# Windowed attention and token/channel mixing on one core: the addition of 1e-9 to the softmax sums moves from VectorE to GpSimd

## The chip, the cores and the metric

The kernel runs on one core of a Trainium2 chip. The metric is the device time of one execution in microseconds (us). A core has five engines that run their own instruction queues in order and wait for one another by semaphores: TensorE (PE in the profile; PEld are its weight loads), VectorE (DVE), ScalarE (ACT), GpSimd (POOL) and SyncE (SP), which here issues most DMAs.

## The reference

Attention with a causal window of 64 over 8 batches, 8 heads, 576 positions and a head size of 64; its output x goes through a token-mixing and a channel-mixing product, each with a residual. All in float32.

```python
scores = scale * np.matmul(q, k.transpose(0, 1, 3, 2))
mask = (rel >= 0) & (rel < window)
scores = np.where(mask, scores, -1000000000.0)
scores = scores - np.max(scores, axis=-1, keepdims=True)
attn = np.exp(scores)
attn = attn / (np.sum(attn, axis=-1, keepdims=True) + 1e-09)
x = np.matmul(attn, v)                     # then heads are joined: batch, position, 512
h = np.maximum(xt @ w_tok1, 0.0) @ w_tok2  # xt: x with positions last
u = x + h.transpose(0, 2, 1)
h2 = np.maximum(u @ w_ch1, 0.0) @ w_ch2
return u + h2
```

## The kernel before

The positions of a batch are cut into nine blocks of 64. A tile is two such blocks, 128 rows for the 128 partitions; there are NT = 36 tiles, nine for each pair of batches, and tile 4 of each nine holds the last block of both batches. The weights arrive as 64-bit floats and are turned into 32-bit ones on the chip, a piece of up to 128x384 at a time (a job). Products that need full precision are done with operands split in two, hi and lo.

The kernel is written in two stages. The first, up to about 290 us, is one loop over i = -1 to 36, in which several tiles are in work at once: scores of tile i+1, softmax of tile i+1, transposition and attention output of tile i, first token product of tile i-1, second token product for earlier tiles, and jobs. The second stage, some 600 us, is the channel product, in which TensorE works almost without a gap. The order on each engine's queue is that of the program text; nothing is reordered.

What an iteration puts on the queues, as far as it bears on the change:

- **VectorE**, in order: softmax(i+1, 0), that is e (L259, scores times scale plus mask) and nm (L262, the negated maximum), or for tiles below 7 only nm (L256) and its scaling (L257); then recip(i) (L297 and L298); the first half of a job's conversion, job_convert_a, L165 to L167 (for i below 4 it stands behind the next softmax half); softmax(i+1, 1); hlo (L345) where a batch's first token product ends; the conversion's second half, L176, L178, L179; and norm(i), x (L303), which multiplies the attention output by the reciprocal ri. For i below 4, norm(i-1) stands ahead of recip(i). In iterations 4 to 6 the weight t2 is split on VectorE too (t2lo, L92), right behind recip(i).
- **GpSimd**, in order: in job_finish the lo part of a weight (t1lo or w1lo, L92), for i below 4 the lo part of an x (split_x, xlo, L92), w (L181, the last addition of a conversion), and from i = 3 on, at the tail of the iteration, split_x of tile i: xlo (L92), or for tile 4 of nine two instructions of L315. split_x waits for ScalarE's hi part, and that for x.
- **ScalarE**: copies of transposed scores (L279), hi parts (L89, L314), the exponentials (L270) with their sums, copies of the token product (L380). softmax_exp(i, 1), which completes the sums of tile i, is issued in iteration i-1, ahead of that iteration's tail.

sm holds the eight sums of each row of a tile (128x8), ri its reciprocals; ri has two buffers. The jobs run in all iterations but those where i mod 9 is 5, and a few listed by hand.

Of the kernel before, what the change touches and what calls it, by code (L numbers as in the profile page):

```python
# [72 lines left out]
def mixer_kernel(ctx: ExitStack, tc: tile.TileContext, qh, kh, vh, wt1, wt2, wc1, wc2, out):  # L73
    nc = tc.nc
# [36 lines left out]
    with ExitStack() as actx:  # L111
# [182 lines left out]
        def recip(i):  # L294
            _, sm = st.pop(i)
            ri = pa.tile([P, H], F32, name=f"ri{i}", tag="ri", bufs=2)
            nc.vector.tensor_scalar_add(ri, sm, 1e-9)  # L297
            nc.vector.reciprocal(ri, ri)  # L298
            return ri

# [135 lines left out]
        for i in range(-1, NT + 1):  # L436
# [24 lines left out]
            if 0 <= i < NT:  # L461
                ri = recip(i)
# [165 lines left out]
```

## Time and profile before

| | |
|---|---|
| time, median of 3 runs | 893.15 us (892.65 to 893.91) |
| the profiled execution, its own time | 894.62 us |
| its span, first to last instruction | 892.5 us |
| mean granted TensorE clock | 0.994 |
| GpSimd busy | 129.3 us (14%) |

The profile is of one execution. Its page gives the busy time of each engine; the span in slices; the chain of work that ended last, followed back from the last instruction; and the costliest groups of instructions by line, with the tile that is written and the one that is read (ri<-sum). A row in order of time starts with the start and the duration in us, then engine, line, operation, tiles and shape; a bracket at its end gives how long the engine had been idle before it and for whom it waited. An instruction can start a few hundredths before the one ahead of it on its engine has ended. A row of the chain gives start, length and what was on the chain then. Busy time of an instruction includes time in which it was started but could not proceed.

### The profile page before, as it was taken

To read this page: it belongs to the slowest core of one execution; us is meant where nothing else is said; L and a number is where in the kernel's file an instruction comes from. 1 tells how busy PE (TensorE), PEld (TensorE's weight loads), DVE (VectorE), ACT (ScalarE), POOL (GpSimd) and SP (SyncE) were. 2 spreads that over 40 slices of the span, in tenths; PEclk is the share of its full clock that TensorE was granted. 3 is DMA by queue.
4 is the path that set the end of the run, shared out by engine and by line. 5 is a ranking of instruction groups with operands and counts; after the bars stand their busy time and mean duration, and the time that the engine had idled before them with its cause. 6 is when DMAs were issued, how large, how long until landed. Compare 5 with 4: busy or idle time off the path is not lost.

```text
span 892.5 us, 14591 instructions
## 1 busy us (share of the span) xinstructions
PE 864.8 (97%) x6002; PEld 706.3 (79%) x6002; DVE 381.5 (43%) x686; ACT 304.9 (34%) x953; POOL 129.3 (14%) x130
## 2 busy tenths in 40 slices
PE   6889999999999979999999999999999999999998
PEld 4667777778778758888888888888888888888887
DVE  4979979988885781130130130220230220220211
ACT  5778778787785240130120120120120120220210
POOL 2434444443332450000000000000000000000000
PEclk9989999999999999999999999999999999999999
DMA  9556667677736330200200200100100100200001
GB/s 324 184 202 242 214 231 241 205 232 261 247 137 196 110 109 24 70 1 24 71 0 32 63 1 35 59 1 36 59 0 36 59 13 24 59 12 35 1 12 36
DMA packets 41490, 87.05 MB, mean 98 GB/s; under 512 B 5456, under 2 KB 19408, under 8 KB 39504
## 3 DMA queue, kind: packets, MB, share of 16 engines
q1 hardware_dynamic: 39312, 84.29, 28.3%
q10 hardware_dynamic: 2112, 1.84, 0.6%
q8 instruction: 47, 0.77, 0.3%
q14 instruction: 19, 0.16, 0.1%
HBM read 65.27 MB, written 20.84 MB: 96 GB/s over the span
## 4 chain that ended last, share of the span: by engine, by line
PE 79%; DVE 14%; ACT 4%; issue 1%; DMA 1%; SPq 0%; POOL 0%; DVEq 0%; ACTq 0%
PE op L586 33%; PE gp L552 30%; PE up L375 4%; PE s L242 3%; PE xp L289 3%; PE h L333 3%; ACT e L270 2%; DVE nm L262 2%; DVE e L259 2%; PE up L368 2%; DVE c L176 2%; PE pp L277 2%; DVE c L165 1%; DVE c L167 1%; ACT pt L279 1%
## 5 line engine op out<-in xcount | busy, mean ns | idle before, releaser
L556 ACT ACTIVATE ghi<-gp 128x512 fp32r<-128x512 f32 x108 | 64.4, 598 | 454.3 <-PE gp L552 453.9
L552 PE MATMUL gp<-uhi,w1hi 128*128 128x512 f32 x432 | 169.1, 392 | 6.4 <-DVE glo L557 6.4
L586 PE MATMUL op<-glo,w2hi 128*128 128x512 f32 (+1 forms) x444 | 170.2, 383 | 0.0
L586 PE MATMUL op<-ghi,w2lo 128*128 128x512 f32 (+1 forms) x444 | 170.2, 383 | 0.0
L586 PE MATMUL op<-ghi,w2hi 128*128 128x512 f32 (+1 forms) x444 | 170.2, 383 | 0.0
L552 PE MATMUL gp<-ulo,w1hi 128*128 128x512 f32 x432 | 168.8, 391 | 0.0
L552 PE MATMUL gp<-uhi,w1lo 128*128 128x512 f32 x432 | 168.7, 390 | 0.0
L557 DVE SCALAR_TENSOR_TENSOR glo<-gp,ghi 128x512 fp32r<-128x512 f32 x108 | 74.4, 690 | 190.4 <-ACT ghi L556 190.3
L588 DVE TENSOR_TENSOR uf<-op,uf 128x512 f32<-128x512 f32 (+1 forms) x37 | 25.1, 677 | 262.2 <-PE op L586 262.2
L552 PEld LDWEIGHTS gp<-uhi,w1hi 128*128 128x128 f32 x432 | 81.5, 189 | 25.2 <-DVE glo L557 8.3
L270 ACT ACTIVATE e<-e,nm 128x128 f32<-128x128 f32 x232 | 90.4, 392 | 25.0 <-DVE nm L262 23.6
L586 PEld LDWEIGHTS op<-glo,w2hi 128*128 128x128 f32 x444 | 83.4, 188 | 16.4
L586 PEld LDWEIGHTS op<-ghi,w2hi 128*128 128x128 f32 x444 | 83.4, 188 | 16.4
L586 PEld LDWEIGHTS op<-ghi,w2lo 128*128 128x128 f32 x444 | 83.4, 188 | 16.4
L552 PEld LDWEIGHTS gp<-uhi,w1lo 128*128 128x128 f32 x432 | 81.5, 189 | 17.0
L552 PEld LDWEIGHTS gp<-ulo,w1hi 128*128 128x128 f32 x432 | 81.4, 188 | 16.8
L181 POOL TENSOR_TENSOR w<-r,c 128x384 f32<-128x384 f32 (+1 forms) x39 | 38.6, 991 | 142.2 <-DVE r L179 116.3
L289 PEld LDWEIGHTS xp<-v,pt 128*64 128x64 f32 x1152 | 39.4, 139 | 21.0 <-ACT pt L279 8.7
L289 PE MATMUL xp<-v,pt 128*64 128x64 f32 x1152 | 47.1, 229 | 5.9 <-ACT pt L279 5.2
L279 ACT COPY pt<-pp 128x512 f32<-128x512 f32 x72 | 41.7, 583 | 14.7 <-PE pp L277 14.5
L242 PE MATMUL s<-k,q 64*64 64x128 f32 x1152 | 44.4, 288 | 1.3 <-DMA k<-kh 0.6
L277 PE MATMUL pp<-ident,e 128*128 128x128 f32 x288 | 45.3, 287 | 0.0
(70 smaller groups left out, 1024.2 us busy)
## 6 DMA issues: line engine op xcount, KB each, us to landing
v<-vh SPq DMA_DIRECT2D x36, 512.0 KB, 3.9
raw<-wc SPq DMA_DIRECT2D x32, 384.0 KB, 4.4
q<-qh SPq DMA_DIRECT2D x36, 256.0 KB, 4.3
k<-kh SPq DMA_DIRECT2D x7, 1280.0 KB, 7.9
out<-uf SPq DMA_DIRECT2D x35, 256.0 KB, 2.3
uf<-u_dram SPq DMA_DIRECT2D x8, 1024.0 KB, 5.8
u_dram<-u SPq DMA_DIRECT2D x7, 512.0 KB, 4.4
w_dram<-w SPq DMA_DIRECT2D x10, 192.0 KB, 3.8
```

The costliest lines, as they stand in the source:

```text
L181: nc.gpsimd.tensor_add(w, rf, cf)
L242: nc.tensor.matmul(s[u][half * BLK:(half + 1) * BLK, j], qt[r, j, half], kbs[b][r, j, n * BLK:n * BLK + P], start=not on_pe, stop=True, sk ...
L270: nc.scalar.activation(e[:, h], src[:, h], AF.Exp, bias=nm[:, g:g + 1], scale=by, accum_out=sm[:, g:g + 1])
L277: nc.tensor.transpose(pp[:, h], e[:, h], ident)
L279: nc.scalar.copy(pt, pp)
L289: nc.tensor.matmul(xp[half * BLK:(half + 1) * BLK, h], pts[h % 2][:, h // 2, half * BLK:(half + 1) * BLK], vt[:, half, h], start=True, sto ...
L333: nc.tensor.matmul(h_ps[b][tt], w[r, slot * DT + tt * P:slot * DT + (tt + 1) * P], x[r], start=first and n == 0, stop=last and n == len(co ...
L375: nc.tensor.matmul(up[:, :n], hx[:, cs], w[:, tt * S + s0:tt * S + s0 + n], start=False, stop=(k == 6), skip_group_check=True)
L552: nc.tensor.matmul(gp, w[:, ct * F + ft * P:ct * F + (ft + 1) * P], x[:, ct], start=(k == 0), stop=(k == 3 * NCT - 1))
L556: nc.scalar.activation(ghi, gp, AF.Relu)
L557: nc.vector.scalar_tensor_tensor(out=glo, in0=gp, scalar=0.0, in1=ghi.bitcast(F32), op0=ALU.max, op1=ALU.subtract)
L586: nc.tensor.matmul(op, w[:, ft, cs], x[:, cols], start=(k == 0), stop=(k == 3 * NFT - 1))
```

## The change

The addition of 1e-9 to the sums is issued on GpSimd; the reciprocal stays on VectorE and now reads what GpSimd wrote. The order in which the program issues the instructions is the same.

```diff
         def recip(i):
             _, sm = st.pop(i)
             ri = pa.tile([P, H], F32, name=f"ri{i}", tag="ri", bufs=2)
-            nc.vector.tensor_scalar_add(ri, sm, 1e-9)
+            nc.gpsimd.tensor_scalar_add(ri, sm, 1e-9)
             nc.vector.reciprocal(ri, ri)
             return ri
```

## The prediction

> **What bounds the kernel now.** I read the page's first parts, then the busy time by stretch, then the line that the change touches, then VectorE (DVE) and GpSimd (POOL) side by side in order of time. From the page: span, PE's busy time, and the chain that ended last by engine.
>
> ```profile
> span 892.5 us, 14591 instructions
> PE 864.8 (97%) x6002; PEld 706.3 (79%) x6002; DVE 381.5 (43%) x686; ACT 304.9 (34%) x953; POOL 129.3 (14%) x130
> PE 79%; DVE 14%; ACT 4%; issue 1%; DMA 1%; SPq 0%; POOL 0%; DVEq 0%; ACTq 0%
> ```
>
> TensorE is the bound on the whole, but 14% of the chain runs over VectorE. The stretches say where (columns: length, then busy time of PE, PEld, DVE, ACT, POOL with their instructions, granted clock, DMA share, GB/s).
>
> ```profile
> 20.00:40.00 20.00, 17.47 (x249) 13.10 (x246) 18.93 (x43) 15.63 (x62) 9.26 (x10) 1.00 0.71 235
> 84.00:114.00 30.00, 29.12 (x365) 23.70 (x368) 28.49 (x54) 22.86 (x88) 13.16 (x13) 1.00 0.63 206
> 146.00:168.00 22.00, 21.26 (x272) 17.23 (x268) 20.86 (x40) 16.94 (x64) 9.00 (x9) 1.00 0.68 238
> 170.00:280.00 110.00, 107.22 (x1338) 86.03 (x1337) 91.29 (x184) 84.39 (x308) 40.09 (x35) 1.00 0.63 207
> ```
>
> From 20 to 40 us VectorE is the fuller engine (95% against 87%): a shorter VectorE helps there. From 84 to 114 and 146 to 168 us both are at about 95% or more: a later VectorE delays TensorE there, an earlier one gains little. From 170 us TensorE (97%) leads and VectorE has 17% of slack. The moved line is in none but these stages. Its own two lines (duration min/median/max in ns):
>
> ```profile
> L297 DVE TENSOR_SCALAR ri<-sum x36: 155/438/922, 14.8 to 271.0; 128x8 f32<-128x8 f32 x36
> L298 DVE RECIPROCAL ri<-ri x36: 202/203/205, 15.0 to 271.6; 128x8 f32<-128x8 f32 x36
> ```
>
> The addition needs 0.155 us and often takes three times that; the reciprocal never takes longer. Iteration i = 12 shows why. In order of time, VectorE, then GpSimd, then the last piece of the sums on ScalarE:
>
> ```profile
> 100.22 0.69 DVE L262 TENSOR_REDUCE nm<-e 128x4 f32<-128x512 f32 x1
> 100.82 0.75 DVE L297 TENSOR_SCALAR ri<-sum 128x8 f32<-128x8 f32 x1
> 101.61 0.20 DVE L298 RECIPROCAL ri<-ri 128x8 f32<-128x8 f32 x1
> 101.73 1.00 DVE L165 TENSOR_SCALAR c<-raw 128x384 int32<-128x384 int32 x1
> 102.76 0.36 DVE L166 TENSOR_SCALAR c<-c 128x384 f32<-128x384 f32 x1
> ...
> 100.25 1.29 POOL L92 TENSOR_TENSOR xlo<-x,xhi 128x512 fp32r<-128x512 f32 x1 [0.25 <-ACT xhi L89]
> 101.50 1.01 POOL L92 TENSOR_TENSOR w1lo<-w,w1hi 128x384 fp32r<-128x384 f32 x1
> ...
> 98.95 0.18 ACT L270 ACTIVATION_READ_ACCUMULATOR e<-e,nm 128x1 f32 x1
> ```
>
> GpSimd's xlo ends at 101.54, and only then does L297 get through (end 101.57). L165 then waits in the same way for w1lo (ends 102.51 and 102.73). The reduction and the reciprocal pass GpSimd unhindered. So most of L297's time is a wait for GpSimd, and that wait doesn't go away by handing the addition to GpSimd: there it stands **behind** the same xlo, because the tail of iteration i-1 issues split_x(i-1) before recip(i) is reached.
>
> **The change part by part.** *The addition on GpSimd.* Its inputs are there: the sums of tile 12 are complete at 99.13, before xlo starts. It can start when the instruction ahead of it ends, even 0.04 us earlier (w1lo starts at 101.50, xlo ends at 101.54). No row shows a 128x8 tensor_scalar on GpSimd, so its cost a is bounded by these (mean ns of one behind the bar):
>
> ```profile
> L92 POOL TENSOR_TENSOR xlo<-x,xhi 128x512 fp32r<-128x512 f32 x32 | 41.3, 1289 | 27.2 <-ACT xhi L89 27.0 <-DVE ri L298 0.3
> L92 POOL TENSOR_TENSOR t1lo<-w,t1hi 128x320 fp32r<-128x320 f32 x4 | 3.5, 869 | 7.2 <-ACT t1hi L89 7.2
> masks.py:199 POOL TENSOR_SCALAR_AFFINE_SELECT ident<-ident 128x128 f32<-128x128 f32 x1 | 0.3, 292 | 0.1
> L615 POOL MEMSET const-float32-0.0<- 128x1 f32 x1 | 0.1, 98 | 0.2 <-issue 0.2
> ```
>
> Below, the memset of one element: 0.10 us. Above, the select over 128 elements: 0.29 us. The two subtractions give (1289-869)/192 = 2.19 ns an element and 169 ns at none, so 186 ns at eight elements. I take a = 0.19, and 0.10 to 0.29 for the range. Less than nothing is out: it is an instruction more on a queue that runs in order.
>
> *The added wait.* The reciprocal now waits for GpSimd. From the end of xlo to the next engine takes 0.05 us (row 41.27 below, after xlo's end at 41.22). With E for the end of xlo, the reciprocal starts at E - 0.04 + a + 0.05 = E + 0.20; it started at E + 0.07. Behind it on VectorE stand the conversion L165 to L167, the second half's softmax, L176 to L179 and x (L303), for which the next xhi, xlo and TensorE wait. Behind the addition on GpSimd stand the split of a weight (w1lo, t1lo) and w (L181); TensorE needs w1lo only in the last stage, so of these only VectorE's own waits for GpSimd count.
>
> *Iterations where w1lo follows at once.* w1lo moves back by a - 0.04 = 0.15 us, and L165, which ends after it, with it: 0.15 later each. Where that lies on the chain of waits, L165 appears in it with its 0.9 us: six times (i = 9, 11, 12, 13, 19, 20), first and last here, and once (i = 18) L166.
>
> ```profile
> 78.26 0.95 DVE c L165
> ...
> 148.19 1.06 DVE c L166
> ...
> 163.99 0.94 DVE c L165
> ```
>
> Six times 0.15 is **+0.90**. At i = 18 the reciprocal comes 0.10 later, and L165 may then lose its place ahead of w1lo, which costs up to a whole L165 (0.3): I take **+0.2**. In the other iterations either nm lasts longer than xlo (0.1 earlier or later, with slack) or TensorE leads: 0.
>
> *Iterations 4 and 5.* Here L297 slips in before xlo has got going, and the addition will have to wait for all of it. VectorE, GpSimd, and the chain's row for TensorE:
>
> ```profile
> 40.12 0.20 DVE L298 RECIPROCAL ri<-ri 128x8 f32<-128x8 f32 x1
> 40.79 0.84 DVE L92 TENSOR_TENSOR t2lo<-w,t2hi 128x384 fp32r<-128x384 f32 x1 [0.47 <-ACT t2hi L89]
> 48.02 1.36 DVE L92 TENSOR_TENSOR t2lo<-w,t2hi 128x384 fp32r<-128x384 f32 x1 [1.31 <-ACT t2hi L89]
> 57.03 0.56 DVE L92 TENSOR_TENSOR t2lo<-w,t2hi 128x384 fp32r<-128x384 f32 x1 [0.28 <-ACT t2hi L89]
> ...
> 39.95 1.27 POOL L92 TENSOR_TENSOR xlo<-x,xhi 128x512 fp32r<-128x512 f32 x1 [0.24 <-ACT xhi L89]
> 47.68 1.28 POOL L315 TENSOR_TENSOR xlo<-x,xlo 64x512 fp32r<-64x512 f32 x1
> ...
> 41.27 1.42 PE h L333 x5
> ```
>
> The reciprocal goes from 40.12 to E + 0.20 = 41.42. t2lo behind it waited for xlo anyway and ended at 41.63, 0.41 after E. Now it starts 0.12 after the reciprocal (as L165 at 101.73 after 101.61) and needs its undisturbed 0.56: E + 0.88. That is 0.47 later, and the same at i = 5 (E = 48.96, end 49.38): **+0.94** together.
>
> *Iterations 0 to 3.* Here recip(i) stands before this iteration's GpSimd work, so the addition is done in time and VectorE is spared 0.19 (27.66 to 27.85). Whether that counts depends on the waits behind it:
>
> ```profile
> 22.19 0.60 DVE L257 TENSOR_SCALAR nm<-nm 128x4 f32<-128x4 f32 x1
> 23.05 1.27 DVE L166 TENSOR_SCALAR c<-c 128x320 f32<-128x320 f32 x1
> 27.66 0.15 DVE L297 TENSOR_SCALAR ri<-sum 128x8 f32<-128x8 f32 x1
> 27.85 0.20 DVE L298 RECIPROCAL ri<-ri 128x8 f32<-128x8 f32 x1
> 28.64 1.17 DVE L257 TENSOR_SCALAR nm<-nm 128x4 f32<-128x4 f32 x1
> 30.08 0.33 DVE L166 TENSOR_SCALAR c<-c 128x320 f32<-128x320 f32 x1
> ...
> 22.71 1.43 POOL L92 TENSOR_TENSOR xlo<-x,xhi 128x512 fp32r<-128x512 f32 x1
> 28.51 1.28 POOL L92 TENSOR_TENSOR xlo<-x,xhi 128x512 fp32r<-128x512 f32 x1
> ```
>
> At i = 2 the scaling L257 comes at 28.64, just after xlo has begun at 28.51, and loses a microsecond. 0.19 earlier it falls before xlo, as at i = 1, where it ended at 22.79 and L166 took the wait instead, ending 0.18 after xlo (24.32 against 24.14). Worked so, xlo ends at about 29.94 and L166 at 30.12 instead of 30.41: 0.29 gained; the same at i = 3. At i = 1 the split ahead of xlo holds L257 either way, at i = 0 VectorE waits for TensorE afterwards: 0. Together **-0.58**.
>
> [...]
>
> *Sum:* 0.90 + 0.20 + 0.94 - 0.58 = **+1.46 us**, on a profiled execution of 894.62 us (span 892.5), which is 0.16% above the median of 893.15. Carried to the median: **894.6**. With a = 0.10: 6 x 0.06 + 2 x 0.38 + 0.1 - 0.58 = +0.6; with 0.29: 6 x 0.25 + 2 x 0.57 + 0.36 - 0.58 = +2.4. So this case's own range is 893.7 to 895.6.
>
> **The rivals.** *The addition is dear.* If one small GpSimd instruction and its signal take about 0.5 us, near the middle between the select's 0.29 and the 0.87 of a 128x320 subtraction, each of the eight places costs 0.31 more and i = 18 its 0.36: +4.1, 897.3. It tips over the 0.2% from a = 0.24 on. For it: no row has this operation. Against: the memset's 98 ns.
>
> *Nothing is gained early.* The wait only moves from L257 to L166 and VectorE's iteration stays as long as it is. For it: at i = 1, where the wait sits on L166 (1.27), VectorE loses as much to GpSimd as at i = 2 on L257 (1.17). Then +2.04: 895.2.
>
> *Iterations 4 and 5 hide it.* If TensorE's h matmuls, which wait for the same xlo (41.27), and not t2lo set the end there, the 0.94 goes: +0.5, 893.7.
>
> *Faster.* If the addition got done before nm ends also in the six iterations, the reciprocal would follow nm at 100.82; L165 would get in at xlo's end as L257 did at 22.79, and L166 would end 0.18 after w1lo, itself pushed from 102.51 by the 0.15 that xlo took longer at 22.71 (1.43, not 1.28), at 102.84 instead of 102.76 + 0.36 = 103.12. Six times 0.28 and the 0.58, without the loss at 4 and 5: -2.2, 891.0. It decides where xlo ends before nm. Against: at i = 12 xlo ends 0.63 after nm, and GpSimd's order is as written.
>
> **How the numbers follow.** 0.2% (1.8 us: below 891.4, above 894.9) is about what this kernel's runs can tell from no change. The forecast case 0.48 (0.28 within the bound, 0.20 above), dear 0.20 (slower), nothing early 0.09 (0.07 slower), hidden 0.11 (within), faster 0.12. Faster 0.12, same 0.41, slower 0.47. The range reaches down to 892.3, between hidden and faster, and up to 897.5, past the dear case.
>
> **What would show it.** On GpSimd 36 instructions of 0.1 to 0.3 us, in iterations 6 to 34 right behind xlo; VectorE's L298 idle before it "<-POOL ri"; at i = 9 to 13 L298 0.1 to 0.2 us after xlo's end and L165 as late; at i = 4 and 5 t2lo at 0.56 us but ending 0.9 after xlo; at i = 2 and 3 L257 at 0.2 to 0.4 us and L166 at over a microsecond. Wrong is the prediction if the additions take 0.4 us or more, if VectorE's iterations from 84 to 114 us get no longer, or if the time moves after 300 us, where nothing was changed.

## The result, and the profile after

The changed kernel takes 902.84 us (median of 4 runs, 901.69 to 903.75), the kernel before 893.53 us beside it (892.65 to 894.79): a ratio of 1.0102 with a 95% interval of 1.0083 to 1.0122. The change costs 9.3 us where 1.5 was forecast, and the time lies above the predicted range. Three single executions among those below (2933.52 us of the kernel before, 1697.85 and 4783.19 us of two kernels with fill, the last of them that kernel's profiled one) ran in a slow state and are left out of the ratios.

From the page of the changed kernel, its span and its engines' busy times:

```profile
span 899.9 us, 14590 instructions
PE 868.0 (96%) x6002; PEld 707.6 (79%) x6002; DVE 367.6 (41%) x650; ACT 304.4 (34%) x953; POOL 138.8 (15%) x166
```

The profiled execution took 901.69 us; against the 894.62 of the profiled execution before it shows 7.07 of the 9.3 us. VectorE has lost 36 instructions and 13.9 us of busy time, and the kernel is longer. Before, the 36 additions were started for 15.6 us in all, where 36 undisturbed ones of 0.155 would take 5.6: most of what VectorE got rid of was time spent started and waiting, and it waits still, now outside an instruction. The two lines of the change, with what VectorE sat idle for ahead of the reciprocal (us, times):

```profile
L297 POOL TENSOR_SCALAR ri<-sum x36: 232/233/237, 13.3 to 280.7; 128x8 f32<-128x8 f32 x36
L298 DVE RECIPROCAL ri<-ri x36: 186/203/204, 14.9 to 281.0; 128x8 f32<-128x8 f32 x36
...
  POOL ri L297: 31.5, 29
```

Those 31.5 us are not the loss: some 10 of them were waited before too, inside L297, and others lie where they cost nothing (2.43 us in iteration 14, whose x is no later than that of 13). The loss is how much later the reciprocal and what follows it come. Iteration 12, VectorE, then GpSimd, in order of time:

```profile
102.34 0.69 DVE L262 TENSOR_REDUCE nm<-e 128x4 f32<-128x512 f32 x1
104.08 0.20 DVE L298 RECIPROCAL ri<-ri 128x8 f32<-128x8 f32 x1 [1.05 <-POOL ri L297]
104.20 1.16 DVE L165 TENSOR_SCALAR c<-raw 128x384 int32<-128x384 int32 x1
...
102.44 1.29 POOL L92 TENSOR_TENSOR xlo<-x,xhi 128x512 fp32r<-128x512 f32 x1 [0.25 <-ACT xhi L89]
103.82 0.23 POOL L297 TENSOR_SCALAR ri<-sum 128x8 f32<-128x8 f32 x1
104.13 1.02 POOL L92 TENSOR_TENSOR w1lo<-w,w1hi 128x384 fp32r<-128x384 f32 x1
```

xlo ends at 103.73 (E). The addition doesn't overlap with it by 0.04 us but comes 0.09 after; it lasts 0.23, and w1lo starts 0.08 after its end. So the reciprocal starts at E + 0.35 (before: E + 0.07) and w1lo at E + 0.40 (before: E - 0.04). L165 waits for w1lo as before (ends at 105.36 and 105.15).

Where the time goes is read from x (L303), once in each iteration on VectorE. Tiles 3, 5, 8, 13, 16, 22, 25 and 35, first before the change:

```profile
38.53 0.68 DVE L303 TENSOR_TENSOR x<-xp,ri 128x512 f32<-128x512 f32 x1
...
53.80 0.69 DVE L303 TENSOR_TENSOR x<-xp,ri 128x512 f32<-128x512 f32 x1
...
75.29 0.68 DVE L303 TENSOR_TENSOR x<-xp,ri 128x512 f32<-128x512 f32 x1
...
113.73 0.69 DVE L303 TENSOR_TENSOR x<-xp,ri 128x512 f32<-128x512 f32 x1
...
137.46 0.68 DVE L303 TENSOR_TENSOR x<-xp,ri 128x512 f32<-128x512 f32 x1
...
183.34 0.68 DVE L303 TENSOR_TENSOR x<-xp,ri 128x512 f32<-128x512 f32 x1
...
205.08 0.68 DVE L303 TENSOR_TENSOR x<-xp,ri 128x512 f32<-128x512 f32 x1
...
276.19 0.69 DVE L303 TENSOR_TENSOR x<-xp,ri 128x512 f32<-128x512 f32 x1 [0.75 <-PE xp L289]
```

And the same tiles after it:

```profile
38.09 0.69 DVE L303 TENSOR_TENSOR x<-xp,ri 128x512 f32<-128x512 f32 x1
...
54.48 0.68 DVE L303 TENSOR_TENSOR x<-xp,ri 128x512 f32<-128x512 f32 x1
...
76.38 0.68 DVE L303 TENSOR_TENSOR x<-xp,ri 128x512 f32<-128x512 f32 x1
...
116.67 0.68 DVE L303 TENSOR_TENSOR x<-xp,ri 128x512 f32<-128x512 f32 x1
...
140.35 0.68 DVE L303 TENSOR_TENSOR x<-xp,ri 128x512 f32<-128x512 f32 x1
...
188.46 0.68 DVE L303 TENSOR_TENSOR x<-xp,ri 128x512 f32<-128x512 f32 x1
...
211.74 0.69 DVE L303 TENSOR_TENSOR x<-xp,ri 128x512 f32<-128x512 f32 x1
...
283.71 0.68 DVE L303 TENSOR_TENSOR x<-xp,ri 128x512 f32<-128x512 f32 x1
```

The differences: -0.44, +0.68, +1.09, +2.94, +2.89, +5.12, +6.66, +7.52 us; the span is 7.4 longer, so nothing is lost after the first stage. In two parts, from tile 8 to 13 and from 16 to 22, 1.85 and 2.23 us are lost: 0.37 in each of 11 iterations. Between tiles 22 and 25 another 1.54 us goes, and there something else is at work. TensorE from 191 us on, then its stretches (columns as before; the granted clock is the third number from the end):

```profile
191.25 0.50 PE L333 MATMUL h<-xhi,t1hi 128*128 128x512 f32 x1 [1.24 <-POOL xhi L315]
...
193.66 1.76 PE L289 MATMUL xp<-v,pt 128*64 128x64 f32 x28 [0.36 <-ACT pt L279]
195.35 1.93 PE L242 MATMUL s<-k,q 64*64 64x128 f32 x32
```

```profile
191.00:193.00 2.00, 1.75 (x6) 0.78 (x6) 0.09 (x1) 1.98 (x10) 1.76 (x4) 1.00 0.98 343
193.00:194.00 1.00, 0.64 (x11) 0.50 (x12) 0.97 (x3) 1.00 (x5) 0.95 (x1) 0.84 1.12 276
194.00:197.00 3.00, 3.00 (x60) 2.82 (x56) 2.19 (x4) 2.77 (x11) 0.07 (x1) 0.50 0.99 301
197.00:199.00 2.00, 2.00 (x25) 1.79 (x17) 1.64 (x4) 0.76 (x2) 1.43 (x2) 0.98 0.79 294
330.30:333.60 3.30, 3.30 (x9) 2.53 (x9) 3.20 (x4) 1.47 (x3) 2.37 (x2) 0.50 0.00 1
```

After a wait of 1.24 us for the split of tile 22 (L315), the clock granted to TensorE falls to half from 193.7 to 197.1 us (the means of 0.84 and 0.98 in the stretches beside it give these ends), and 32 score matmuls take 1.93 us instead of 1.10. The kernel before had no such stretch there. It had one at 49 to 57 us and one at 323 to 326, where the changed kernel has them too (the latter at 330 to 334, last row), so those cost nothing in the comparison.

### The profile page after: what moved, and what is told of

The parts are those of the page before. It is cut to its first block, busy times and chain, and to the rows that moved or that the text cites. A ratio compares the mean times of both kernels' runs of the same rounds, so it can differ in the third digit from the quotient of the medians.

```text
span 899.9 us, 14590 instructions
## 1 busy us (share of the span) xinstructions
PE 868.0 (96%) x6002; PEld 707.6 (79%) x6002; DVE 367.6 (41%) x650; ACT 304.4 (34%) x953; POOL 138.8 (15%) x166
## 4 chain that ended last, share of the span: by engine, by line
PE 68%; DVE 5%; ACT 1%; issue 1%; POOL 1%; ACTq 0%; DVEq 0%; POOLq 0%
PE op L586 33%; PE gp L552 30%; PE up L375 2%; DVE c L176 1%; PE up L368 1%; DVE c L167 1%; PE xp L289 1%; ACT e L270 1%; PE h L333 1%; DVE glo L557 0%; DVE c L165 0%; DVE c L166 0%; DVE r L179 0%; PE s L242 0%; PE pp L277 0%
## 5 line engine op out<-in xcount | busy, mean ns | idle before, releaser
L279 ACT COPY pt<-pp 128x512 f32<-128x512 f32 x72 | 41.6, 583 | 13.9 <-PE pp L277 13.6
L92 POOL TENSOR_TENSOR xlo<-x,xhi 128x512 fp32r<-128x512 f32 x32 | 41.6, 1300 | 25.7 <-ACT xhi L89 25.7
```

Of the source, the lines that this page charges most:

```text
L92: eng_lo.tensor_sub(lo, src, hi.bitcast(F32))
L279: nc.scalar.copy(pt, pp)
```

## The experiments

The question was which part of 9.3 us comes from the later reciprocal, which from the work added to GpSimd, and which from TensorE's clock. All were timed in five rounds against the kernel before on the same chip; intervals are 95%.

**The instruction without the wait.** VectorE keeps its addition, and GpSimd makes the same one into a tile that nobody reads.

```diff
             nc.vector.tensor_scalar_add(ri, sm, 1e-9)
+            spare = pa.tile([P, H], F32, name=f"spare{i}", tag="spare", bufs=2)
+            nc.gpsimd.tensor_scalar_add(spare, sm, 1e-9)
             nc.vector.reciprocal(ri, ri)
```

> The addition stays on VectorE as before; GpSimd makes a second one, in the same place of its queue, into a tile that nobody reads. Theory 1 (the wait: VectorE's reciprocal stands still until GpSimd has ended xlo and then run the addition alone): VectorE no longer waits for an addition, only w1lo comes some 0.4 us later and L165 with it, by 0.2 us in six to ten iterations: 1.2 to 2 us over the kernel before, no gap in iterations 14, 23, 32. [...]

Measured: 894.23 us, 0.9996 (0.9984 to 1.0008): no loss, not even the 1.2 to 2 us that were expected of the later w1lo. Iteration 12, VectorE, then GpSimd:

```profile
102.92 0.20 DVE L300 RECIPROCAL ri<-ri 128x8 f32<-128x8 f32 x1
103.04 0.31 DVE L165 TENSOR_SCALAR c<-raw 128x384 int32<-128x384 int32 x1
...
101.56 1.29 POOL L92 TENSOR_TENSOR xlo<-x,xhi 128x512 fp32r<-128x512 f32 x1 [0.24 <-ACT xhi L89]
102.94 0.45 POOL L299 TENSOR_SCALAR spare<-sum 128x8 f32<-128x8 f32 x1
103.47 1.14 POOL L92 TENSOR_TENSOR w1lo<-w,w1hi 128x384 fp32r<-128x384 f32 x1
```

xlo ends at 102.85; w1lo starts 0.62 after it, later than in the change, and it costs nothing: VectorE's reciprocal is where it was (E + 0.07), and L165 gets through in the gap. GpSimd's load and its later weight split are not what is paid for.

**No addition at all.** This kernel leaves out the addition of 1e-9; the reciprocal reads the sums.

```diff
-            nc.vector.tensor_scalar_add(ri, sm, 1e-9)
-            nc.vector.reciprocal(ri, ri)
+            nc.vector.reciprocal(ri, sm)
```

> Leaves out the addition of 1e-9: the reciprocal reads the sums directly, on VectorE, and GpSimd has nothing of it. Theory 1: the reciprocal no longer stands behind GpSimd's xlo, VectorE saves 0.2 to 0.3 us in each iteration where it is the fuller engine: 1 to 2.5 us under the kernel before. Rival: VectorE's length counts for nothing where TensorE is at 97%: within 0.5 us of the kernel before.

Measured: 894.91 us, 1.0000 (0.9986 to 1.0014). This missed the 1 to 2.5 us that were expected: not even leaving the line out gains anything in the median. Its trace says where the gain went (table below): tile 22 comes 4.1 us earlier than before, tile 25 only 2.3 and tile 35 only 0.7. It loses it in stretches of half clock at 184 to 188 and 253 to 257 us.

**The addition one place earlier on GpSimd**, ahead of the tail's split of x, so that it stands before xlo in the queue.

```diff
+        def add_eps(i):
+            ris[i] = pa.tile([P, H], F32, name=f"ri{i}", tag="ri", bufs=3)
+            nc.gpsimd.tensor_scalar_add(ris[i], st[i][1], 1e-9)
...
+            if i + 1 < NT:
+                add_eps(i + 1)
             # tail of iteration i: split_x(i)
```

> GpSimd makes the addition, but one place earlier on its queue: at the end of iteration i-1, ahead of the split of x that it stood behind. The same 36 instructions on the same engine. Theory 1: the sums are there and the addition is done before VectorE gets to the reciprocal, so the loss is gone: -2 to +1 us against the kernel before; xlo comes up to 0.15 us later. [...]

Measured: 895.54 us, 1.0005 (0.9992 to 1.0019): the loss is gone. GpSimd and VectorE, iteration 12:

```profile
100.23 0.23 POOL L298 TENSOR_SCALAR ri<-sum 128x8 f32<-128x8 f32 x1
100.54 1.29 POOL L92 TENSOR_TENSOR xlo<-x,xhi 128x512 fp32r<-128x512 f32 x1
...
101.42 0.19 DVE L303 RECIPROCAL ri<-ri 128x8 f32<-128x8 f32 x1
```

The same 36 instructions, on the same engine, 0.23 us each; the reciprocal follows nm without a wait, 0.41 before xlo's end (101.83). The place in the queue decides.

**Another operation in the same place:** an addition of two tiles, the operation that xlo and w1lo are, with a tile of 1e-9.

```diff
-            nc.gpsimd.tensor_scalar_add(ri, sm, 1e-9)
+            nc.gpsimd.tensor_add(ri, sm, eps)      # eps: 128x8, set once to 1e-9
```

> As the change, but GpSimd adds a tile that holds 1e-9 in every element (tensor_tensor, the same operation as xlo and w1lo) instead of a constant. In the changed kernel's trace the addition starts 0.08 us after xlo's end and w1lo 0.08 us after the addition, where w1lo starts 0.04 us before xlo's end in the kernel before. If the change of operation makes these gaps, they close, the addition costs some 0.25 us less in each iteration, and the time is 4 to 6 us over the kernel before. If something else makes them, it is as long as the change or a little longer, 9 us over.

Measured: 901.26 us, 1.0067 (1.0049 to 1.0086). GpSimd and VectorE in an iteration of the same kind:

```profile
86.71 1.29 POOL L92 TENSOR_TENSOR xlo<-x,xhi 128x512 fp32r<-128x512 f32 x1 [0.25 <-ACT xhi L89]
87.95 0.20 POOL L300 TENSOR_TENSOR ri<-sum,eps 128x8 f32<-128x8 f32 x1
88.11 1.02 POOL L92 TENSOR_TENSOR w1lo<-w,w1hi 128x384 fp32r<-128x384 f32 x1
...
88.19 0.20 DVE L301 RECIPROCAL ri<-ri 128x8 f32<-128x8 f32 x1 [0.89 <-POOL ri L300]
88.31 1.04 DVE L168 TENSOR_SCALAR c<-raw 128x384 int32<-128x384 int32 x1
```

In this iteration the prediction's picture holds to 0.01 us: the addition lasts 0.20 (a = 0.19), starts 0.05 before xlo's end (88.00), w1lo 0.11 after it, the reciprocal at E + 0.19 (predicted E + 0.20). And the waits then cost what was forecast: by tile 22 it has lost 1.0 us against its own start (table). Another 3.5 us come from there to tile 35, of which 1.2 from tile 23 to 24 and 1.6 from 31 to 33, in stretches of half clock, and 1.6 us more behind 300 us, where this execution has two such stretches (324 to 327 and 334 to 338 us) and the kernel before one. So the kernel is 6.6 us over the one before although its waits up to tile 22 cost no more than was forecast.

The start of x in us, less that of the kernel before, for the profiled executions; what a kernel loses or gains is its difference from its own first row:

| tile | changed | two-tile addition | no addition | reciprocal behind L167 (below) | the same with fill (below) |
|---|---|---|---|---|---|
| 0 | +0.16 | +1.05 | +0.25 | -1.23 | -0.23 |
| 3 | -0.44 | +0.42 | -0.23 | -1.83 | -0.85 |
| 5 | +0.68 | +1.34 | -0.26 | -1.71 | -0.71 |
| 9 | +1.44 | +1.34 | -2.37 | -2.20 | -2.86 |
| 13 | +2.94 | +1.71 | -3.33 | -3.25 | -3.92 |
| 22 | +5.12 | +2.05 | -4.09 | -3.91 | -4.56 |
| 24 | +6.50 | +3.41 | -2.36 | -3.40 | -4.05 |
| 31 | +6.96 | +3.69 | -2.39 | -3.32 | -3.97 |
| 33 | +7.41 | +5.26 | -0.94 | -1.66 | -3.67 |
| 35 | +7.52 | +5.57 | -0.66 | -1.37 | -3.56 |

**The change in part of the iterations.** Tile 4 of each nine is split in two instructions of L315, and some of the longest waits of TensorE stand behind them, in the next iteration (i mod 9 = 5). One kernel makes the change everywhere else, one there alone.

```diff
+            (nc.vector if i % TPP == 5 else nc.gpsimd).tensor_scalar_add(ri, sm, 1e-9)   # everywhere else
```

> GpSimd adds in all iterations but those where i mod 9 is 5 (5, 14, 23, 32); there VectorE does. Theory 1 (the wait): the loss of 0.37 us an iteration from 9 to 13 and 18 to 22 stays, and that of iteration 4: 4 to 5 us over the kernel before. With the clock (the changed kernel's TensorE ran at half clock once more, from 193 to 197 us, after the wait of iteration 23): this stretch at half clock is gone, and nothing of the 2 us between tiles 23 and 24 is left. Rival (no part of the loss hangs on iterations 5 and 23): 8 to 9 us.

```diff
+            (nc.gpsimd if i % TPP == 5 else nc.vector).tensor_scalar_add(ri, sm, 1e-9)   # there alone
```

> GpSimd adds only in iterations 5, 14, 23 and 32, where its queue holds two halves of xlo ahead of the addition. VectorE's reciprocal waits 1.5 to 2.9 us there. Theory 1 by the wait alone: iteration 5 costs 0.5 us, the others are hidden by ScalarE and TensorE: 0.5 us over the kernel before. With the clock: if the wait of iteration 23 alone makes TensorE drop to half clock, 2 to 3 us over, and a stretch of 4 us at half clock near 190 us.

Measured: everywhere else 901.59 us, 1.0089 (1.0068 to 1.0109); there alone 897.22, 1.0024 (1.0008 to 1.0040). The first was a miss: the half-clock stretch at 191 us stayed, though iteration 23's own addition was on VectorE. TensorE waited there for the same xhi (L315) just as long, 1.26 us: by then VectorE was late from iterations 17 to 22. In the second, iteration 5 loses 0.56 us (from tile 4 to 5), as it does in the change; the half-clock stretch moved to 55 to 62 us and cost 1.3 more than before; 14, 23 and 32 lose nothing that lasts. By the wait alone 0.5 us was expected there, so most of the 2.8 us is not the wait.

**TensorE kept busy.** In the kernel before, the transposes of one half of iteration 5 are made three times. In the changed kernel likewise, and the scores of one half are made three times at i = 23 (the last ones count).

```diff
-            for h in range(4):
-                nc.tensor.transpose(pp[:, h], e[:, h], ident)
+            for _ in range(3 if (i, u) == (5, 1) else 1):
+                for h in range(4):
+                    nc.tensor.transpose(pp[:, h], e[:, h], ident)
```

> The kernel before with the same doubled work in iteration 5 alone: three times four transposes, 0.85 us of work into a wait of 1.16 us. If the wait makes the clock drop, the stretch at half clock from 49 to 57 us is gone or shorter and the kernel is 1.5 to 3.5 us faster than before; otherwise it is the same or 0.5 us slower.

> The changed kernel, and TensorE does some work twice in two places where it waits for GpSimd's halves of xlo: the four transposes of the second half three times in iteration 5, the second half's scores three times in iteration 23 (the same values into the same place). If the waits make the clock drop, one or both stretches at half clock (50 to 57 us, 193 to 197 us) are gone, and the kernel is 1.5 us faster for the second and up to 3 us for the first than the changed one: 5 to 8 us over the kernel before instead of 9. If the clock drops for another reason, both stay, and the time is that of the change or up to 1 us more.

The kernel before with fill: 893.8 us, 0.9993 (0.9982 to 1.0004). In its profiled execution the first stage has no stretch at half clock (the one at 321 to 325 us stays). First the kernel before, then this one, 49 to 57 us:

```profile
49.00:57.00 8.00, 7.19 (x76) 5.72 (x75) 7.48 (x16) 4.97 (x18) 2.28 (x2) 0.57 0.61 229
```

```profile
49.00:57.00 8.00, 6.23 (x81) 4.38 (x80) 7.76 (x18) 5.85 (x23) 2.30 (x2) 1.00 0.63 221
```

More matmuls, less busy time, and from tile 6 on everything is 1.7 us earlier to the end. But it doesn't happen in each execution, so that the median hardly moves, and single runs of the kernel before are as short without any fill (892.4 us at the same mean clock of 0.998). The changed kernel with fill: 902.82 us, 1.0091 (1.0071 to 1.0112), no gain in the median; in its profile the stretch at 194 us is gone (tiles 22 to 25: 6.04 to 6.02 us late, where the change went from 5.12 to 6.66) and that at 50 us stayed. A second stretch behind 300 us, at 334 to 338, takes the gain back: the lateness grows from 6.91 us at tile 35 to 8.2 at the end. From 195 us:

```profile
195.54 1.10 PE L242 MATMUL s<-k,q 64*64 64x128 f32 x32
```

**The reciprocal later on VectorE.** The addition stays on GpSimd in the change's own place; the reciprocal moves behind L165 to L167 and the second softmax half, ahead of L176. All of the reference is computed.

```diff
             nc.gpsimd.tensor_scalar_add(ri, sm, 1e-9)
-            nc.vector.reciprocal(ri, ri)
...
             softmax_exp(i + 1, 1)
+            if 0 <= i < NT:
+                nc.vector.reciprocal(ri, ri)
```

> The changed kernel with the addition where the change has it on GpSimd, and only the reciprocal moved down VectorE's queue: behind the first half of the conversion and the second half's softmax, ahead of L176, so that nothing waits behind it. Theory 1 (the loss is VectorE's wait, and the conversion and softmax stuck behind it): the loss is gone, -2 to +1 us against the kernel before, L298 never idles. Rival (the later w1lo on GpSimd counts by itself): 2 us or more remain.

> The changed kernel once more, for the spread of its times over the mean granted clock of TensorE. If part of its loss is the clock, its runs fall into groups by clock (0.989, 0.992, with luck 0.994 and above), 1.5 to 3 us apart, and at the same clock as a run of the kernel before it is some 6 us longer instead of 9. If the loss is all waiting, the clock doesn't sort the times.

Measured: 893.97 us, 0.9996 (0.9987 to 1.0006), where the changed kernel, run again beside it, took 902.7, 1.0096 (1.0077 to 1.0115). The runs of the latter do sort by mean granted clock, 901.11 to 902.85 at 0.992, 903.0 at 0.989 and 906.86 at 0.985, but none came at 0.994 or above, where nearly all runs of the kernel before lie, so they can't be compared at equal clock. GpSimd and VectorE, iteration 12:

```profile
97.47 1.29 POOL L92 TENSOR_TENSOR xlo<-x,xhi 128x512 fp32r<-128x512 f32 x1 [0.24 <-ACT xhi L89]
98.85 0.27 POOL L297 TENSOR_SCALAR ri<-sum 128x8 f32<-128x8 f32 x1
99.20 1.11 POOL L92 TENSOR_TENSOR w1lo<-w,w1hi 128x384 fp32r<-128x384 f32 x1
...
98.68 0.35 DVE L165 TENSOR_SCALAR c<-raw 128x384 int32<-128x384 int32 x1
101.76 0.19 DVE L487 RECIPROCAL ri<-ri 128x8 f32<-128x8 f32 x1
```

GpSimd does the same as in the change, with the same gaps, and the loss is gone: L165 starts before w1lo has begun, right behind nm, and the reciprocal finds its operand done. What the waits lose was VectorE's wait at the reciprocal, which held up L165 and all that stands behind it.

**Fill, with the better placings.** Transposes of one half three times at i = 5, twice at 23 and 32, in the early kernel, in the one that leaves out the addition, and in the late one; and in the changed kernel five times at 5, three times at 32, with the scores of fill at 23.

```diff
-            for h in range(4):
-                nc.tensor.transpose(pp[:, h], e[:, h], ident)
+            for _ in range({(5, 1): 3, (23, 1): 2, (32, 1): 2}.get((i, u), 1)):
+                for h in range(4):
+                    nc.tensor.transpose(pp[:, h], e[:, h], ident)
```

> The addition on GpSimd one place earlier on its queue, and TensorE transposes the second half three times in iteration 5 and twice in iterations 23 and 32, where it waits for GpSimd's halves of xlo. If the two causes (the wait and the clock) are right, it has neither: no stretch at half clock, 1 to 3 us under the kernel before.

> Leaves out the addition of 1e-9, with the same doubled transposes. In the kernel without the addition VectorE was 4.1 us ahead of the kernel before at tile 22 and lost it again in two stretches at half clock (184 to 188, 253 to 257 us). If these go, 2.5 to 4 us under the kernel before; if they come for another reason than TensorE's waits, within 1 us of it.

> The changed kernel with more doubled work on TensorE: the transposes of the second half five times in iteration 5 and three times in iteration 32, the second half's scores three times in iteration 23. It holds TensorE's clock up and leaves VectorE's wait as it is. If the wait alone is worth 6 us and the clock the rest, its runs at full clock are 6 us over the runs of the kernel before at full clock, and the median is 6 to 7.5 us over. If the clock has no share of its own, the median stays 8.5 us or more over.

> The kernel with the reciprocal further down VectorE's queue (all of the reference computed), with TensorE's transposes of the second half three times in iteration 5 and twice in iterations 23 and 32. If wait and clock are the two causes it has neither: 2 to 3 us under the kernel before, with a mean granted clock of 0.996 to 0.998. If not, it stays within 1 us of it.

| kernel | median us | ratio (95%) | runs by mean granted clock, us |
|---|---|---|---|
| before (with the last two) | 894.31 | | 0.998: 892.37 to 892.56; 0.990: 896.88 |
| early, fill | 893.96 | 1.0010 (0.9996 to 1.0024) | 0.996: 893.13 to 893.48; 0.990: 897.28 to 898.85 |
| no addition, fill | 891.9 | 0.9978 (0.9961 to 0.9995) | 0.998: 889.49 to 891.55; 0.990: 896.05, 896.44 |
| changed, fill | 903.6 | 1.0084 (1.0061 to 1.0107) | 0.998: 898.87; 0.991: 903.56 to 903.67 |
| late, fill | 892.15 | 0.9984 (0.9970 to 0.9998) | 0.998: 890.83 to 891.02; 0.992: 895.28, 895.41 |

Within these kernels the time goes with the clock: 4 to 7 us lie between the runs at the highest and at the lowest. It isn't so in all: of the two-tile addition the run at the lowest clock, 0.985, was the shortest (899.24 us). At the same 0.998 the changed kernel with fill is 898.87 (one run; with the first fill it has one too, 898.58) against 892.37 to 892.56: about 6.4 us are lost with equally little half clock in both, a single stretch of 3.4 us by the mean (half of 3.4 is 0.2% of 892). As an estimate, from two runs with fill, that leaves some 3 of the 9.3 us for the clock. The profiled pair agrees on the waits: 7.4 us less the 1.54 of the stretch at 194 us is 5.9. The fill doesn't keep the stretches away from each run of the changed kernel, and its medians don't move.

By the ratios the kernel without the addition gains 2.0 us with fill where 2.5 to 4 were expected, the late one 1.4 where 2 to 3 were, and the early one missed its 1 to 3 us altogether. The profiled execution of the early one has no half-clock stretch in the first stage, but two between 315 and 328 us. Each trace read here has one there, at the start of the second stage, and five have two: early, the two-tile addition, and with fill the early kernel, the changed one (first fill) and the one without the addition. In these five 1.3 to 1.7 us are lost between tile 35 and the end, in the others at most 0.2. So part of what fill gains in the first stage goes into a second stretch in the second stage.

The late kernel with fill computes all of the reference and is 0.16% faster than the kernel before, at the edge of what can be told. Its profiled execution has a span of 889.0 us and a single half-clock stretch, at 319 to 323; without the fill the late kernel had two more, at 47 to 55 us (clock 0.57) and at 252 to 257 (0.66).

## Why the prediction was wrong, step by step

Three steps failed: the size of what the small instruction holds up on GpSimd, the number of iterations in which that counts, and TensorE's clock, which the sum put at nothing.

**The first failing step, the size,** is "It can start when the instruction ahead of it ends, even 0.04 us earlier", with a = 0.19. The overlap was read from w1lo behind xlo, two subtractions of one kind. A tensor_scalar between them shows no overlap but a gap of 0.08 to 0.09 us on both sides, and 0.23 of its own: w1lo goes back by 0.44 where 0.15 was worked out. Put into the prediction's formula (w1lo moves by a - 0.04), that is a = 0.48, although the instruction's duration lies within the range of 0.10 to 0.29. The range bounded the duration and not what the instruction holds up. The two-tile addition shows that the rest of the working on the waits was sound: with its 0.20 and its overlap, 1.0 us was lost by tile 22 against 1.46 in the sum. It shows too that this step alone doesn't make the miss: that kernel still took 901.26 us, above the predicted range, and in its profiled execution 4.4 us of that went in half-clock stretches. What makes the gap inside GpSimd no run shows; that it goes with the kind of operation does the comparison of the two.

**The second, the count: six times 0.15, where L165 lies "on the chain of waits".** 0.37 us are lost in each of 11 iterations, 8 to 13 and 16 to 22, also where L165 wasn't on the chain. Both kernels fit a slack of about 0.07 per iteration, which is inferred and not read: 0.44 less 0.07 is 0.37, and the two-tile addition's 0.15 lost 0.09 in each of tiles 9 to 13. The chain of before shows what is late now; a delay longer than the slack puts the other iterations on it as well, tiles 21 and 22 behind 170 us among them. Together 4.1 us stand in place of 1.1 (the 0.90 and the 0.20).

**Iterations 4 and 5** were right in kind: +0.94 predicted, +1.12 measured (tile 3 to 5). VectorE and GpSimd at i = 4:

```profile
41.13 0.20 DVE L298 RECIPROCAL ri<-ri 128x8 f32<-128x8 f32 x1 [1.55 <-POOL ri L297]
41.25 0.51 DVE L92 TENSOR_TENSOR t2lo<-w,t2hi 128x384 fp32r<-128x384 f32 x1
...
39.51 1.27 POOL L92 TENSOR_TENSOR xlo<-x,xhi 128x512 fp32r<-128x512 f32 x1 [0.24 <-ACT xhi L89]
40.86 0.23 POOL L297 TENSOR_SCALAR ri<-sum 128x8 f32<-128x8 f32 x1
```

xlo ends at 40.78 and t2lo at 41.76, 0.98 after it (predicted 0.88; before 0.41), now undisturbed as forecast. The rival by which TensorE hides it falls. Tiles 5 to 8 lose 0.41 more, which the sum didn't have.

**Iterations 0 to 3** were right: -0.58 predicted; -0.60 measured, from +0.16 at tile 0 to -0.44 at tile 3. L257 at i = 2 takes 0.17 us instead of 1.17, and L166 behind it takes the wait with 1.28. The rival by which nothing is gained early falls.

**The third, the clock,** stands in none of the terms: TensorE's rate was taken as given. The half-clock stretch between tiles 22 and 25 costs 1.54 us in the profiled execution, and the clock some 3 us in the median by the estimate above; in the two-tile addition it is most of what is lost. The trace of before had such a stretch already (0.57 in the mean over 49 to 57 us), between the stretches that the prediction read. Why the changed kernels get more of them stays open.

**From 170 us on**, zero was predicted for want of a VectorE wait that counts. From tile 25 to 35, 0.86 us are lost, 0.09 an iteration, at full clock: VectorE's 17% of slack didn't hide the delay wholly. Through which wait it comes no run tells.

**The dear rival** ("one small GpSimd instruction and its signal take about 0.5 us") had in effect the mechanism that came out (what the instruction holds up, though not its duration) and a chance of 0.20, but counted eight places (897.3), where VectorE loses the full amount in eleven besides 4 and 5, and no clock. The faster rival's arithmetic, that VectorE gains about 0.28 in an iteration once nothing waits for xlo, is what the late kernel shows (tiles 9 to 13: 1.05 us, 0.26 each); there the median keeps none of it, as the gain goes into half-clock stretches, and part of it with fill.

That nothing moves after 300 us was right for the profiled execution: the lateness of tile 35 (7.52) is that of the span (7.4).

## What to carry to other kernels

A cheap instruction that is handed to an in-order queue costs what stands ahead of it there plus the gaps around it (here up to 1.29 us of xlo, and 0.08 to 0.09 on both sides), and its reader pays: look for the place in that queue first (ahead of xlo, or with its reader later), since the same 36 instructions cost 9 us in one place and nothing in two others. Price it with a neighbour of another kind of operation, not with two like ones, and multiply by all iterations whose slack is smaller than the delay. Where TensorE's granted clock dips in the profile, give the dips a term and a range of their own, and compare kernels at equal clock before explaining a difference of a few us.

## What of the hardware was not expected

- In the changed kernel a 128x8 tensor_scalar on GpSimd lasts 0.23 us (232 to 237 ns in all 36) and holds back the next subtraction by 0.44 (iteration 12); in the two-tile addition a 128x8 tensor_tensor lasts 0.20 and holds it back by 0.15 (row 87.95). In the late kernel the tensor_scalar took 0.27 (row 98.85), with the spare tile 0.45 (row 102.94).
- TensorE's granted clock falls to 0.50 for stretches of 3.4 or 6.8 us, at 1.2 to 1.7 us each; in the profiled executions of before and after it is 0.50 or 1.00 and nothing else, and a value between them is a mean over a mixed stretch. In the clock records of these two the starts lie on a grid of 3.413 us: in the changed kernel 50.33, 193.69 and 330.22 us, 42 and 40 steps apart; in the kernel before 49.70 and 322.77 us, 80 steps apart. The first stretch of each lasts 6.827 us, two steps, the others 3.413. In neither trace is a wait of TensorE behind the first 25 us longer than 2.54 us: a stretch began some 2.4 us after a single wait of 1.24 us (191.25), and no longer wait stands near it.
- What brings a stretch on remains open. In the late kernel with fill none came behind a wait of 1.58 us (at 52.11 us; the clock is 1.00 in each us from 50 to 100), and in the kernel without the addition one came at 184 with no single wait above 0.42 us from 176 us on. In the changed kernel TensorE was busy for 0.61 of the step of the grid ahead of the stretch at 193.69 us (2.08 of 3.41 us), but a step with 0.50, from 319.98 us (1.70 of 3.41), was not followed by one. Transposes made three times over at i = 5 went with a stretch's absence in the kernel before (clock 1.00 from 49 to 57 us) and not in the changed one (0.76 in the mean over 46 to 60 us). That a busy TensorE prevents them is the author's reading, and no run shows it. The starts also lie elsewhere against the kernel's own work in another execution (49.70 and 50.33 us for the first), and whether that decides it no run shows either.
- The runs of a kernel sort by these stretches, if roughly: those of the kernel before that ran beside the last two kernels, by a granted clock of 0.998, 0.994 and 0.990 into 892.4 to 892.6, 892.6 to 895.4, and 896.9 us.
